# New tables of steps for a group's slots and for the prologue's sums, another order at the beginning, and the last low part of h ahead of the first output tile

## The chip, the cores and the metric

The kernel runs on one core of one Trainium2 chip. The metric is the device time of one execution in microseconds (us). Five engines work side by side, each through its own queue of instructions in program order: TensorE (PE, matmuls), VectorE (DVE), ScalarE (ACT), GpSimd (POOL) and SyncE (SP, which here issues every DMA). An instruction that waits holds up all that stands behind it on its engine.

## The reference

```python
xn = layernorm(x)                                  # x: 2048 x 576
q, k, v = split(xn @ wqkv)                         # 32 heads of 18
scores = q @ k.T * 18 ** -0.5                      # a key counts if 0 <= i - j < 256
s = (softmax(scores) @ v) @ wo
h = (xn @ w_gate) * (xn @ w_up)                    # 4608 columns
g = silu(h @ w_down)
out = x + s * g
```

All of it is float32.

## The kernel before

Each float32 operand is split into a high and a low float16 part, and each product is made of three passes (high x high, high x low, low x high). In the code `hi` writes a high part (ACT) and `lo` a low part (DVE). The parts are scaled by powers of two that come from the largest values.

**The prologue** (about 0 to 178 us). Sixteen tiles of 128 rows of x are normalised: `stats` (DVE), `root` (ACT), `newton` (DVE), then `norm2` (two ACT steps, then two POOL steps in `parts`), then `turn`, a transposing DMA into XT. Tile 0 goes another way: PE transposes it, ACT copies it (`turned`), POOL makes its low part (`turned_low`). `v_pass(t, i0, i1)` makes passes i0 to i1 of the fourteen that give v for tile t, and `v_out` reads them out. The weights of v lie in `rv` (raw) and `wv` (high parts 0 to 4, low parts 5 to 9). The weights of q and k arrive in `rqk` in five blocks. Their largest value `am_qk` is spread over the partitions through PE (`spread_pe`, `spread_pe2`), and `qk_scale` and `qk_split` make the parts that the tiles of q and k (`qk_tile`, L387) need. All this is done for rows 0 to 1023 and then for 1024 to 2047.

**The main part** (about 178 to 1511 us). It has 18 groups of four slots. A group holds 256 of the 4608 columns; a slot works on 512 rows. In a slot, PE makes seven sums of products (q = 0 to 6, L1159, a fast scheme in which sums and differences of blocks of the weights, `tw`, and of x, `sx`, save an eighth of the matmuls), 92 matmuls in 16 places. `h_hi` and `h_lo` split h, the product of both branches, into `hh`. `down` 0 to 4 (L1023) multiplies the h of the slot before by w_down. A step of attention runs in every slot from slot 1 to slot 64, some of it in the slots after: `score` (DVE), `shifted` and `probs` (ACT), `turn_probs` (the low part of the probabilities, then one transposing DMA to `pt`), `weigh` (PE, L940), `finish` (DVE), `finish2` (POOL), `store_o`. `turn_probs(i)` comes in two halves, j = 0 and 1, and the DMA goes out with the second. For the first 16 steps the window has fewer keys.

In each group the weights of the next one are made ready: `ffn_raw` (loads), `ffn_amax` (ACT), the scales, `up_hi`/`up_lo`, `dn_hi`/`dn_lo`/`dn_low`, `wd_sum`/`wd_hi`/`wd_lo`, and `t_sum` (POOL), `t_hi` (ACT), `t_lo` (DVE), which make `tw`.

**What sets the order.** The schedule is written by hand. `at(slot, place, f, ...)` puts a step on a list, and `at_place` issues the steps of a place in the order of their entry, with `score_pairs` and `down` first. In every slot, `seven_place` issues the matmuls of the place before that. The table `AT` gives the places, counted from the first slot of a group (or from the step's own slot) in units of a sixteenth of a slot; a number above 15 lies in a later slot. Negative numbers, relative to slot 0, lie in the prologue's second half.

`AT["p"]` has, for each slot of a group and each of eight quarters of a step, the places of `score`, `shifted`, `probs`, `turn_probs` and `weigh`. `AT["en"]` says for each slot which of ten steps run on DVE (1) rather than POOL (0): the two products of `seven_mult`, then the eight `turn_probs`. `AT["eng"][4]` says where `dn_low` runs, ACT (1) or POOL (0). `AT["on"]` says the same (DVE or POOL) for the steps of `sx`, `AT["sx"]` their places; `t0`, `u0`, `wd0` and `g0` are the places for group 0, made in the prologue.

In the last slot the second part of h is special:

```python
at(sl, (17, 18)[ft] if last else AT["h"][sl % NCH][1][ft], h_lo, sl, ft)
...
at(NSLOT, 1, o_out, 0)
```

so the last two `h_lo` are at places 1 and 2 after the last slot. `o_out(t)` makes output tile t: a silu on ACT (L1250), 28 matmuls (L1262), two DVE steps that read them (L1264), an addition and a store.

Of the kernel before, what the change touches and what calls it, by code (L numbers as in the profile page):

```python
# [13 lines left out]
OP = mybir.AluOpType  # L14
# [6 lines left out]
def kernel(  # L21
# [23 lines left out]
    scale = DH ** -0.5  # L45
# [143 lines left out]
    def hi(w, rv, s):  # L189
        nc.scalar.activation(w, rv, AF.Copy, scale=s)  # L190
# [92 lines left out]
    def turn(t):  # L283
        nc.sync.dma_start(XT[:, :, t * 128:(t + 1) * 128], XN.pop(t), transpose=True)
# [464 lines left out]
    for k in range(3, 5):  # L749
        raw_wide(rqk, wqkv, 0, 2 * D, k)  # L750
# [18 lines left out]
    turned_low(0, nc.gpsimd)  # L769
# [513 lines left out]
    at(NSLOT, 1, o_out, 0)  # L1283
# [41 lines left out]
```

## Time and profile before

| | us |
|---|---|
| runs of the kernel, median (lowest to highest of 3) | 1578.68 (1578.66 to 1579.19) |
| the profiled execution, its own time | 1580.56 |
| its span, first to last instruction | 1578.8 |
| PE busy | 1556.4 (99%) |
| DVE busy | 1268.3 (80%) |
| ACT busy | 1069.4 (68%) |
| POOL busy | 847.7 (54%) |

The granted clock of TensorE was 0.999 over the span. The profile gives one execution. A row of a timeline holds the start, the time taken, the engine, the source line, the operation, out<-in, shapes and count. In brackets follows the idle time of the engine just before it and what ended that. A busy PE is not PE at its peak, since matmuls are pipelined and each record covers the pipeline too. In the chain of work a row holds start, time and what it was. PE reads no waits of its own from a table: only where its row has a bracket did it stand still.

### The profile page before, as it was taken

To read this page: it belongs to the slowest core of one execution; us is meant where nothing else is said; L and a number is where in the kernel's file an instruction comes from. 1 tells how busy PE (TensorE), PEld (TensorE's weight loads), DVE (VectorE), ACT (ScalarE), POOL (GpSimd) and SP (SyncE) were. 2 spreads that over 40 slices of the span, in tenths; PEclk is the share of its full clock that TensorE was granted. 3 is DMA by queue.
4 is the path that set the end of the run, shared out by engine and by line. 5 is a ranking of instruction groups with operands and counts; after the bars stand their busy time and mean duration, and the time that the engine had idled before them with its cause. 6 is when DMAs were issued, how large, how long until landed. Compare 5 with 4: busy or idle time off the path is not lost.

```text
span 1578.8 us, 40055 instructions
## 1 busy us (share of the span) xinstructions
PE 1556.4 (99%) x15498; PEld 1106.7 (70%) x15498; DVE 1268.3 (80%) x2752; ACT 1069.4 (68%) x1853; POOL 847.7 (54%) x1064
## 2 busy tenths in 40 slices
PE   8999999999999999999999999999999999999999
PEld 5465577777777776777777777777777777777767
DVE  7537688888888988898889888888888888877654
ACT  6435478777777877777778787878777777752230
POOL 4126355657464757575766666566757575732000
PEclk9999999999999999999999999999999999999999
DMA  9583436565557687777777676767686868651238
GB/s 233 190 246 129 166 73 138 96 129 107 122 106 143 122 146 137 130 143 135 145 122 152 121 155 119 154 121 149 118 158 123 155 120 149 122 98 38 63 82 220
DMA packets 566575, 212.14 MB, mean 134 GB/s; under 512 B 504560, under 2 KB 544624, under 8 KB 566384
## 3 DMA queue, kind: packets, MB, share of 16 engines
q1 hardware_dynamic: 566384, 209.58, 64.2%
q8 instruction: 121, 1.98, 0.6%
q14 instruction: 70, 0.57, 0.1%
HBM read 76.63 MB, written 29.00 MB: 67 GB/s over the span
## 4 chain that ended last, share of the span: by engine, by line
PE 83%; DVE 6%; POOL 4%; DMA 3%; ACT 2%; issue 2%; SPq 1%; DVEq 0%; POOLq 0%; ACTq 0%
PE up L1159 40%; PE dn L1023 21%; PE s L387 4%; PE pv L940 3%; PE up L1112 3%; PE s L896 2%; PE s L1023 2%; PE s L1262 2%; DMA pt<-pp 2%; PE up L1262 2%; PE up L387 1%; POOL pp L928 1%; DVE hh L1007 1%; POOL tf L507 1%; PE s L338 1%
## 5 line engine op out<-in xcount | busy, mean ns | idle before, releaser
L1023 PE MATMUL dn<-dnw,hh 128*128 128x512 f16 (+1 forms) x3168 | 444.7, 286 | 1.2
L1159 PEld LDWEIGHTS <-tw 128*128 128x128 f16 x3456 | 320.2, 98 | 62.1 <-DVE tw L193 5.1
L1023 PEld LDWEIGHTS <-hh 128*128 128x128 f16 x3456 | 222.2, 98 | 170.8 <-issue 19.2
L1159 PEld LDWEIGHTS <-upw 128*128 128x128 f16 x3024 | 283.8, 98 | 64.5 <-issue 22.2
L1129 DVE SCALAR_TENSOR_TENSOR gt<-up,gt 128x512 f32<-128x512 f32 x360 | 247.7, 688 | 62.4 <-PE up L1112 40.3
L1030 DVE SCALAR_TENSOR_TENSOR acc<-dn,sc,acc 128x512 f32<-128x512 f32 x310 | 215.3, 694 | 99.2 <-PE dn L1023 99.0
L1159 PE MATMUL up<-XT,upw 128*128 128x256 f16 x2160 | 276.6, 273 | 0.0
L915 ACT ACTIVATE mx<-mx,sig 128x2 f32<-128x2 f32 x256 | 98.1, 383 | 217.5 <-DVE mx L907 217.5
L1159 PE MATMUL up<-XT,tw 128*128 128x256 f16 x1728 | 236.0, 273 | 2.5 <-DVE gt L1129 2.5
L1159 PE MATMUL up<-sx,tw 128*128 128x256 f16 x1728 | 225.0, 273 | 2.4 <-DVE tw L193 2.4
L1134 POOL TENSOR_TENSOR ht<-gt 128x512 f32<-128x512 f32 x72 | 92.0, 1278 | 94.7 <-DVE gt L1129 93.9
L940 PEld LDWEIGHTS <-pt 128*128 128x128 f16 x2880 | 109.5, 96 | 41.1 <-DMA pt<-pp 6.3
L940 PE MATMUL pv<-vt,pt 128*128 128x37 f16 x2880 | 112.9, 179 | 4.5 <-DMA pt<-pp 4.5
L1159 PE MATMUL up<-sx,upw 128*128 128x256 f16 x864 | 112.7, 273 | 0.0
L1125 ACT ACTIVATE gt<-up 128x512 f32<-128x512 f32 x144 | 83.7, 581 | 30.9 <-PE up L1159 17.3
L1001 ACT ACTIVATE hh<-ht 128x512 f16<-128x512 f32 x72 | 45.2, 627 | 67.4 <-POOL ht L1134 67.4
L507 POOL TENSOR_TENSOR tf<-raw 128x256 f32<-128x256 f32 x102 | 83.0, 814 | 0.1
L507 POOL TENSOR_TENSOR tf<-raw,tf 128x256 f32<-128x256 f32 x68 | 62.0, 913 | 21.8 <-DVE tw L193 21.8
L193 DVE SCALAR_TENSOR_TENSOR upw<-raw,sc,upw 128x640 f16<-128x640 f32 x72 | 71.9, 1001 | 0.0
L315 ACT ACTIVATE upw<-raw 128x1280 bf16<-128x1280 f32 (+1 forms) x51 | 62.5, 1225 | 3.8 <-DMA raw<-in_B_w_up_dram 3.7
L193 DVE SCALAR_TENSOR_TENSOR tw<-tf,sc,tw 128x512 f16<-128x512 f32 x68 | 49.5, 749 | 14.5 <-ACT tw L190 13.7
L896 PE MATMUL s<-ks,qs 54*128 54x384 f16 (+2 forms) x512 | 60.2, 312 | 0.0
(1353 smaller groups left out, 2918.3 us busy)
## 6 DMA issues: line engine op xcount, KB each, us to landing
raw<-in_B_w_down_dram SPq DMA_DIRECT2D x36, 288.0 KB
qk_d<-qp SPq DMA_DIRECT2D x18, 512.0 KB
raw<-in_B_w_gate_dram SPq DMA_DIRECT2D x36, 256.0 KB
raw<-in_B_w_up_dram SPq DMA_DIRECT2D x36, 256.0 KB
ks<-qk_d SPq DMA_DIRECT2D x96, 81.0 KB
qs<-qk_d SPq DMA_DIRECT2D x128, 54.0 KB
vt<-v_d SPq DMA_DIRECT2D x48, 111.0 KB
qk_d<-qp SPq DMA_DIRECT2D x20, 256.0 KB
```

What stands on the lines that cost most here:

```text
L193: nc.vector.scalar_tensor_tensor(w, rv, s, h, op0=OP.mult, op1=OP.subtract)
L387: nc.tensor.matmul(ps, a, b, start=i == 0 and not opened, stop=i == 12 and opened)
L507: nc.gpsimd.tensor_tensor(t[:, to], x0, x1, op=OP.subtract)
L896: nc.tensor.matmul(ps[:, :hi_ - lo_], QS[s][r, i * 128:(i + 1) * 128], KS[s][r, lo_:hi_], start=True, stop=True)
L915: nc.scalar.activation(mx[:, 1], mx[:, 0], AF.Identity, bias=sig[:, 2:3], scale=sig[:, 1:2])
L940: nc.tensor.matmul(PVB[s][:, j, i, :VW], pt[:, nb * j + n + n // nb * nb], VT[s][:, lo_ + n % nb, j * VW:(j + 1) * VW], start=n == 0, stop ...
L1023: nc.tensor.matmul(to, a, b, start=q == 0, stop=q == len(l) - 1)
L1030: nc.vector.scalar_tensor_tensor(d, src, SC[g][:, 9:10], d, op0=OP.mult, op1=OP.add)
L1125: nc.scalar.activation(seven_new(sl, name), CH[q], AF.Copy, scale=H_SC)
L1129: nc.vector.scalar_tensor_tensor(seven_new(sl, name), CH[q], H_SC, x, op0=OP.mult, op1=OP.add)
L1134: eng.tensor_tensor(HT[sl, f], u[:, 0], u[:, 1], op=OP.mult)
L1159: nc.tensor.matmul(CH[q][:, o], a, b, start=CH["first"], stop=last and q not in (1, 2, 5), skip_group_check=q in ON)
```

## The change

Nearly all entries of `AT` are changed. Those that the steps below speak of, old above new (for `p`, the places of `turn_probs` and `weigh` are the last two of five; only rows of slot 0 and 1 of a group are shown):

```diff
-           "dn": ((41, 45), (51, 52), (52, 48)),
+           "dn": ((37, 45), (51, 54), (52, 48)),
-           "down": ((6, 9, 12, 15, 20), (6, 8, 11, 14, 16), (6, 8, 11, 14, 16), (6, 9, 12, 15, 19)),
+           "down": ((6, 9, 12, 15, 21), (6, 8, 11, 14, 16), (6, 8, 11, 14, 16), (6, 9, 12, 15, 18)),
-           "en": ((0, 1, 0, 0, 0, 0, 1, 0, 0, 0), (0, 1, 0, 0, 0, 0, 1, 0, 0, 0),
-                  (0, 1, 0, 0, 0, 0, 1, 0, 0, 0), (0, 1, 0, 0, 0, 0, 1, 0, 0, 0)),
+           "en": ((0, 1, 0, 0, 0, 0, 0, 1, 0, 0), (0, 1, 0, 0, 0, 0, 1, 1, 0, 0),
+                  (0, 1, 0, 0, 0, 0, 1, 1, 0, 0), (0, 1, 0, 0, 0, 0, 1, 1, 0, 0)),
-           "end": ((30, 32, 35), (28, 32, 33), (28, 32, 33), (28, 32, 33)),
+           "end": ((29, 31, 32), (30, 33, 35), (28, 32, 35), (28, 30, 33)),
-           "eng": (1, 1, 0, 1, 1, 0, 1, 0, 0, 0, 0, 0, 0, 1),
+           "eng": (1, 1, 1, 1, 0, 0, 0, 0, 1, 0, 1, 0, 1, 1),
-           "h": (((15, 17), (18, 21)), ((15, 17), (19, 21)), ((15, 17), (21, 21)), ((15, 17), (19, 21))),
+           "h": (((15, 17), (18, 19)), ((15, 19), (19, 21)), ((15, 17), (20, 21)), ((15, 17), (21, 21))),
-           "p": (((6, 7, 8, 11, 22), (6, 7, 8, 12, 22), (7, 8, 12, 13, 22), (7, 8, 12, 13, 23),
-                  (13, 14, 15, 18, 24), (13, 14, 15, 19, 24), (13, 15, 20, 21, 30), (15, 17, 20, 21, 30)),
-                 ((6, 7, 8, 11, 22), (6, 7, 8, 12, 22), (7, 8, 12, 13, 22), (7, 8, 12, 13, 23),
-                  (13, 14, 15, 18, 24), (13, 14, 15, 19, 24), (13, 15, 20, 21, 28), (15, 17, 20, 21, 28)),
+           "p": (((6, 7, 8, 13, 20), (6, 7, 9, 13, 21), (7, 8, 12, 13, 21), (7, 8, 12, 13, 22),
+                  (13, 14, 15, 18, 25), (13, 14, 15, 19, 25), (13, 15, 20, 21, 29), (15, 17, 20, 21, 29)),
+                 ((6, 7, 8, 11, 22), (6, 7, 8, 12, 22), (7, 8, 10, 13, 24), (7, 8, 10, 13, 25),
+                  (13, 14, 15, 18, 26), (13, 14, 15, 19, 26), (13, 15, 20, 21, 30), (15, 17, 20, 21, 30)),
...
-           "raw": (8, 9, 12, 16, -6, 0),
+           "raw": (7, 9, 16, 17, -5, -1),
-           "sum": ((30, 36, 50, 59, 64), (41, 53, 56, 61, 62)),
+           "sum": ((32, 39, 46, 59, 67), (43, 53, 56, 61, 62)),
-           "t_hi": ((57, 57), (67, 69)),
+           "t_hi": ((57, 57), (70, 70)),
-           "u0": ((-9, -8, -7, -7), (-7, -7, -7, -4)),
+           "u0": ((-9, -8, -7, -7), (-7, -7, -7, -1)),
-           "up_lo": (41, 40, 65, 62),
+           "up_lo": (41, 40, 64, 62),
-           "wd": ((55, 56), (65, 69), (70, 74)),
+           "wd": ((55, 56), (65, 71), (69, 74)),
```

`amax`, `g0`, `load`, `scale`, `sx`, `on`, `t0`, `up_hi` and `wd0` change too, most by one or two places, with a few steps of `sx` on the other of their two engines. The beginning:

```diff
     for k in range(2, 5):
         hi(wv[:, k], rv[:, k], ps_v[:, 2:3])
+    nc.gpsimd.tensor_scalar(rv[:, 0], rv[:, 0], ps_v[:, 2:3], None, op0=OP.mult)
+    nc.gpsimd.tensor_tensor(wv[:, 5], rv[:, 0], wv[:, 0], op=OP.subtract)
     newton(2, 1, 1)
     norm2(3)
     turn(3)
+    stats(4)
+    stats(5)
+    root(4, 2)
     for k in range(1, 3):
         raw_wide(rqk, wqkv, 0, 2 * D, k)
...
-    turned(0, x32[:, 0:4], x32[:, 4])
...
-    stats(4)
-    lo(wv[:, 5], rv[:, 0], ps_v[:, 2:3], wv[:, 0])
-    stats(5)
-    root(4, 2)
+    newton(4, 2)
     lo(wv[:, 6], rv[:, 1], ps_v[:, 2:3], wv[:, 1])
-    newton(4, 2)
     for t in range(4, 6):
         norm2(t)
         turn(t)
-    for k in range(3, 5):
-        raw_wide(rqk, wqkv, 0, 2 * D, k)
...
     stats(6)
+    root(6, 1)
+    newton(6, 1)
+    norm2(6)
+    turn(6)
+    for k in range(3, 5):
+        raw_wide(rqk, wqkv, 0, 2 * D, k)
     v_out(0)
     stats(7)
-    root(6, 2)
+    root(6, 1, 1)
     v_pass(3, 0, 14)
-    newton(6, 2)
-    norm2(6)
-    turn(6)
-    amax(am_qk[:, 0:1], rqk[:, 0])
     v_out(1)
+    newton(6, 1, 1)
     norm2(7)
     turn(7)
+    amax(am_qk[:, 0:1], rqk[:, 0])
+    turned(0, x32[:, 0:4], x32[:, 4])
     turned_low(0, nc.gpsimd)
```

The largest value of q's and k's weights is now spread during `v_pass(7)` (after passes 2 and 5) instead of during `v_pass(6)` (after passes 9 and 12). And at the end:

```diff
-    at(NSLOT, 1, o_out, 0)
+    at(NSLOT, 2, o_out, 0)
```

With that, `o_out(0)` comes after both `h_lo` and after `down` 4 of the slot before the last.

More of the change, by code (lines that the diff above doesn't have):

```diff
@@ L66 @@
     LEAST, MOST = 2.0 ** -60, 2.0 ** 60
-    AT = {"amax": (19, 20, 6),
-           "dn": ((41, 45), (51, 52), (52, 48)),
-           "down": ((6, 9, 12, 15, 20), (6, 8, 11, 14, 16), (6, 8, 11, 14, 16), (6, 9, 12, 15, 19)),
-           "en": ((0, 1, 0, 0, 0, 0, 1, 0, 0, 0), (0, 1, 0, 0, 0, 0, 1, 0, 0, 0),
-                  (0, 1, 0, 0, 0, 0, 1, 0, 0, 0), (0, 1, 0, 0, 0, 0, 1, 0, 0, 0)),
-           "end": ((30, 32, 35), (28, 32, 33), (28, 32, 33), (28, 32, 33)),
-           "eng": (1, 1, 0, 1, 1, 0, 1, 0, 0, 0, 0, 0, 0, 1),
-           "g0": (-22, -19, -22, -21, -9, -16, -14, -11, -11),
-           "h": (((15, 17), (18, 21)), ((15, 17), (19, 21)), ((15, 17), (21, 21)), ((15, 17), (19, 21))),
-           "load": (8, 3, 15),
-           "mult": {1: 6, 4: 18, 5: 1, 6: 0},
[12 rows of a table removed]
-           "pairs": (6, 13),
-           "raw": (8, 9, 12, 16, -6, 0),
-           "scale": (26, 28, 35, 51),
-           "sum": ((30, 36, 50, 59, 64), (41, 53, 56, 61, 62)),
[5 rows of a table removed]
-           "t_hi": ((57, 57), (67, 69)),
-           "t_lo": ((57, 58), (70, 71)),
-           "u0": ((-9, -8, -7, -7), (-7, -7, -7, -4)),
-           "up_hi": (36, 36, 60, 61),
-           "up_lo": (41, 40, 65, 62),
-           "wd": ((55, 56), (65, 69), (70, 74)),
-           "wd0": ((-4, 3), (-1, 4), (-1, 7))}
@@ new lines @@
+    AT = {"amax": (18, 20, 6),
+           "dn": ((37, 45), (51, 54), (52, 48)),
[4 more added lines that the diff above has]
+           "eng": (1, 1, 1, 1, 0, 0, 0, 0, 1, 0, 1, 0, 1, 1),
+           "g0": (-22, -22, -20, -23, -10, -15, -14, -11, -11),
+           "h": (((15, 17), (18, 19)), ((15, 19), (19, 21)), ((15, 17), (20, 21)), ((15, 17), (21, 21))),
+           "load": (7, 3, 14),
+           "mult": {1: 6, 4: 20, 5: 1, 6: 0},
[12 rows of a table added]
+           "pairs": (6, 13),
+           "raw": (7, 9, 16, 17, -5, -1),
+           "scale": (25, 28, 35, 50),
+           "sum": ((32, 39, 46, 59, 67), (43, 53, 56, 61, 62)),
[5 rows of a table added]
+           "t_hi": ((57, 57), (70, 70)),
+           "t_lo": ((57, 58), (70, 71)),
+           "u0": ((-9, -8, -7, -7), (-7, -7, -7, -1)),
+           "up_hi": (37, 37, 61, 61),
+           "up_lo": (41, 40, 64, 62),
+           "wd": ((55, 56), (65, 71), (69, 74)),
+           "wd0": ((-4, 0), (-1, 6), (-1, 7))}
@@ L779 @@
         if t % 8 > 3 or t >= 8:
-            v_pass(t, 0, 9)
-            if t == 6:
+            v_pass(t, 0, 2)
+            if t == 7:
                 spread_pe(am_qk[:, 5:6], 1, "s", 4)
-            v_pass(t, 9, 12)
-            if t == 6:
+            v_pass(t, 2, 5)
+            if t == 7:
                 tp = spread_pe2(1, "s", 4)
-            v_pass(t, 12, 14)
-            if t == 6:
                 qk_scale(tp)
+            v_pass(t, 5, 14)
             if t == 6:
```

26 rows, old and new, of the table AT are left out of this document.

## The prediction

> **What bounds the kernel now.** I read the page first, then who makes PE wait, then the chain of work, then the timelines of single engines at each place where PE waits.
>
> ```profile
> span 1578.8 us, 40055 instructions
> PE 1556.4 (99%) x15498; PEld 1106.7 (70%) x15498; DVE 1268.3 (80%) x2752; ACT 1069.4 (68%) x1853; POOL 847.7 (54%) x1064
> ```
>
> PE runs one fixed stream of matmuls, and the change leaves their number alone. So the change can only move the time through the gaps in that stream. Who made PE wait (total us, times, longest):
>
> ```profile
> PE pv L940 <- DMA pt<-pp: 4.5, 5, 1.1
> PE up L1159 <- DVE gt L1129: 2.5, 2, 2.1
> PE up L1159 <- DVE tw L193: 2.4, 8, 0.4
> PE s L1023 <- DVE hh L1007: 1.5, 2, 1.3
> ```
>
> These idle times are lower bounds. A matmul's record covers its pipeline, so the loss in cadence is some 0.15 us more for each wait. The waits fall in four places: the beginning (its rows follow), one wait of 2.1 us in the first slot, the first of the four slots of a group (tw, pt, and a little hh), and the last slot (the 1.3 of hh). In the chain of work the same 36 matmuls of slot 2 recur:
>
> ```profile
> 1034.48 3.93 PE up L1159 x36
> 1110.06 3.93 PE up L1159 x36
> 45.61 11.22 PE s L387 x52
> 33.03 4.98 DMA XT<-xh
> ```
>
> A group takes 1110.06 - 1034.48 = 75.58 us. One 512-column matmul takes 11.22/52 = 0.216 us. "Same" below means within 0.2% (3.2 us), about what a measurement of this kernel tells from no change.
>
> **The beginning.** PE, DVE, SP and POOL between 18 and 40 us:
>
> ```profile
> 23.82 0.41 PE L338 MATMUL up<-wv,XT 128*128 128x288 f16 x2 [1.34 <-DVE wv L193]
> 29.68 3.60 PE L338 MATMUL s<-wv,XT 128*128 128x288 f16 x28 [0.56 <-DVE sm L262]
> 38.06 2.38 PE L338 MATMUL s<-wv,XT 128*128 128x288 f16 x18 [1.35 <-DMA XT<-xh]
> 22.96 1.54 DVE L193 SCALAR_TENSOR_TENSOR wv<-rv,ps_v,wv 128x576 f16<-128x576 f32 x2
> 26.22 2.87 SPq L284 DMA_TRANSPOSE XT<-xh  x2
> 29.14 0.58 SPq L197 DMA_DIRECT2D rqk<-in_A_wqkv_dram  x1
> 21.16 1.27 POOL L735 TENSOR_TENSOR wv<-rv,wv 128x576 f16<-128x576 f32 x1
> 39.09 0.15 DVE L804 TENSOR_REDUCE am_qk<-am_qk 128x1 f32<-128x5 f32 x1
> ```
>
> Three waits can go: 1.34 + 0.56 + 1.35 = 3.25 us idle, some 3.7 in cadence.
>
> First, PE waits at 23.82 for the low parts of `wv` that start at 22.96. The change takes `lo(wv[:, 5])` (half of that row's two: 0.77 us) off DVE's queue ahead of them, and the rest of that queue (statistics 4 and 5, `newton(4,2)`, the low part of `wv[:, 6]`) is only put in another order. They should come 0.8 to 1.3 us earlier, the upper end if the rows beside POOL's 1.27 are not stretched as now.
>
> POOL gets two operations for it. One like the row of L735 is 1.27 us; the scaling before it is bounded by the same row and by twice that. They fit between POOL's work on tiles 2 and 3 and cost nothing there. Without that cover tile 3 would be late by 1.3 us.
>
> Second, ACT drops the three copies of `turned(0)` from the stretch ahead of tiles 4 and 5, and their statistics are taken sooner. Their normalisation, and the transposes of 26.22, move forward by about 2 us, which ends the wait of 29.68 (an XT tile, I read it, though the view names DVE).
>
> Third, `turn(6)` is now issued ahead of the loads of `rqk` 3 and 4 (29.14 on) instead of behind them. In the chain it is the 4.98 us transfer that PE meets at 38.06, and it should now land before it is wanted.
>
> What is late next: tile 7. Its `norm2` stands behind `v_out(1)` and its transpose behind the two moved loads. I expect it to land near 38.5 to 39.5, against about 38 when PE could want it (tile 6 starts at 38.06 and takes 3.6, less the 3.7 won), so PE waits about 1 us there. Then `am_qk`: before, it was ready at 39.2. With `rqk` 3 and 4 loaded later and `turned(0)` now on ACT ahead of its squares, I expect 39.5 to 40. The change moves its consumer to tile 7, so nine passes of matmuls still cover it.
>
> Sum: 3.7 less about 1.5 = **-2.2 us**, so L387 starts near 43.4 instead of 45.61. Bounds: -4 (no new wait) to +1 (`am_qk` 3 us late). The first slot's wait stays as it is:
>
> ```profile
> 186.03 2.59 PE L1159 MATMUL up<-XT,tw 128*128 128x256 f16 x12 [2.11 <-DVE gt L1129]
> ```
>
> DVE's queue ahead of that read (`dn_lo`, three steps of `sx` for c = 2, one split) keeps its order in the new tables: 0. The step of c = 3 that leaves DVE for POOL, and `up_lo` 3 that comes in at place -1, both lie before an idle stretch of DVE.
>
> **Slot 0 of a group.** Twelve groups lose time here (eight tw waits and four of the five pt waits). One of them:
>
> ```profile
> 998.54 0.48 DVE L1030 SCALAR_TENSOR_TENSOR acc<-dn,sc,acc 128x256 f32<-128x256 f32 x1 [0.27 <-PE dn L1023]
> 998.94 1.12 DVE L928 TENSOR_TENSOR pp<-sm__16025,pp 128x384 f16<-128x384 f32 x1
> 999.99 1.40 DVE L1007 SCALAR_TENSOR_TENSOR hh<-hh,ht 128x512 f16<-128x512 f16 x1
> 1001.31 0.68 DVE L1007 SCALAR_TENSOR_TENSOR hh<-hh,gt 128x512 f16<-128x512 f16 x1
> 999.61 1.23 POOL L928 TENSOR_TENSOR pp<-sm__16025,pp 128x384 f16<-128x384 f32 x1
> 1000.73 1.75 PE L1023 MATMUL dn<-dnw,hh 128*128 128x512 f16 x6
> 1038.99 1.47 PE L1023 MATMUL dn<-dnw,hh 128*128 128x512 f16 x6
> 1004.42 0.35 DVE L193 SCALAR_TENSOR_TENSOR wd<-raw,sc,wd 64x128 f16<-64x128 f32 x1
> 1006.55 0.38 PE L1159 MATMUL up<-sx,tw 128*128 128x256 f16 x2
> 1007.23 0.61 PE L1159 MATMUL up<-sx,tw 128*128 128x256 f16 x4 [0.30 <-DVE tw L193]
> ```
>
> The six matmuls take 1.75 against 1.47 in slot 2: 0.28 lost to `h_lo`. The two at 1006.55 end their issue 2 x 0.11 (3.93/36) later, so the next should start at 1006.77, not 1007.23: 0.46 lost to `t_lo`. With a small follower that is some 0.85 us a group.
>
> The new table puts the second half of `turn_probs(2)` on DVE (now POOL, 1.23 us). It also puts `wd_lo` 0 (0.35) ahead of `h_lo`, and brings `down` 4 one place earlier, which takes DVE's 0.27 of waiting away. Ahead of `h_lo` DVE gains one 128x384 subtraction and 0.35. Beside POOL that subtraction took 1.12, and `h_lo` took 1.40 instead of 0.68.
>
> With POOL's piece gone from that moment, 0.72 comes back on `h_lo` and about 0.4 on the subtraction beside it. So +0.7 (estimate: 1.12 less the 0.4) + 0.35 - 0.27 - 0.72 - 0.4 = about -0.3: `h_lo` no later, slightly earlier. The Trainium skill, "SBUF — State Buffer", section "Who interferes with whom", says that a VectorE instruction with two SBUF inputs and a GpSimd instruction that reads SBUF exclude each other for the whole of whichever began first. The two rows agree (DVE's 1.40 covers the rest of POOL's 1.23 and then its own 0.68), and by the rule moving the piece off POOL is worth slightly more than I take.
>
> Behind `h_lo`, `t_lo` loses the 0.35 of `wd_lo` that stood before it. `t_hi` of both kinds, now at place 6 after ACT's copy, still ends about 1003.2, before DVE wants it. So `t_lo` comes 0.38 earlier or more.
>
> I take **-0.55 us a group, 12 groups: -6.6**; bounds -0.9 and, if DVE is late, +1.0 each. The groups with a pt wait show this:
>
> ```profile
> 627.00 0.47 PE L940 MATMUL pv<-vt,pt 128*128 128x37 f16 x12 [1.04 <-DMA pt<-pp]
> 620.62 2.22 SPq L931 DMA_TRANSPOSE pt<-pp  x1
> ```
>
> The transpose goes out when POOL's piece has ended. On DVE that end is about 0.6 earlier, the same gain. The fifth pt wait is in slot 1, where `weigh(2)` moves one place later: **-0.5**.
>
> **Slots 1 to 3.** These now have slack and lose some. `turn_probs` on DVE rises by one in slots 2 and 3.
>
> ```profile
> 1038.37 0.69 DVE L1007 SCALAR_TENSOR_TENSOR hh<-hh,gt 128x512 f16<-128x512 f16 x1
> 1056.97 0.68 DVE L1007 SCALAR_TENSOR_TENSOR hh<-hh,gt 128x512 f16<-128x512 f16 x1
> 1057.64 1.47 PE L1023 MATMUL dn<-dnw,hh 128*128 128x512 f16 x6
> 1054.91 1.53 DVE L193 SCALAR_TENSOR_TENSOR dnw<-raw,sc,dnw 128x576 f16<-128x576 f32 x2
> L1134 POOL TENSOR_TENSOR ht<-gt 128x512 f32<-128x512 f32 x44 | 55.9, 1271 | 4.1 <-DVE gt L1129 3.3 <-DMA raw<-in_B_w_gate_dram 0.8
> ```
>
> The second `h_lo` ends at 1039.06 in slot 2, and its first matmul (the sixth) is due at 1038.99 + 5 x 0.216 = 1040.07: slack 1.0. In slot 3 it is 1058.72 - 1057.65 = 1.07. The added subtraction is 0.5 to 1.1. In slot 3 one of the two `dn_lo` (1.53/2 = 0.77) moves behind `h_lo` and pays for it.
>
> `dn_low` (two a group) moves from ACT to POOL. Nothing of before shows it there; by size the row of L1134 gives 1.27 x 576/512 = 1.43, and a smaller tile gives less. Its cover is POOL's idle time, and its danger is that DVE waits beside it. In slot 1 `weigh(1)` comes a place earlier, closer to its transpose. I allow **+1.5 us** over all groups; bounds 0 (the slack holds) to +15 (the first rival below has the mechanism: some 1.2 us in each of 12 groups).
>
> **The end.**
>
> ```profile
> 1516.70 0.52 DVE L1264 SCALAR_TENSOR_TENSOR acc<-dn,sig,acc 128x288 f32<-128x288 f32 x1 [2.09 <-ACT acc L1250]
> 1518.35 0.69 DVE L1007 SCALAR_TENSOR_TENSOR hh<-hh,gt 128x512 f16<-128x512 f16 x1
> 1519.09 4.97 PE L1023 MATMUL s<-dnw,hh 128*128 128x512 f16 x43 [1.27 <-DVE hh L1007]
> ```
>
> The last `h_lo` starts at 1518.35 because it is queued on DVE behind `o_out(0)`, whose first step waited 2.09 us for ACT. With `o_out(0)` at place 2, `h_lo` 1 comes first, ends near 1515.4, and `o_out(0)`'s matmuls and `down` 4 cover it. The whole of PE's wait (1.3 us idle, 1.4 in cadence) goes, and all behind it is PE: **-1.4**, within 0.3.
>
> **Sum.** -2.2 + 0 - 6.6 - 0.5 + 1.5 - 1.4 = -9.2 us. The profiled execution took 1580.56 (span 1578.8), so it would be 1571.4. The median of the runs is 1578.68, 1.9 lower, so I forecast 1569.5.
>
> **Rivals.**
>
> *DVE becomes the bound (slower).* The subtraction costs its 1.12, `dn_low` on POOL blocks DVE in slot 3 for up to 2 x 1.43, and `h_lo` comes later than the slack. It decides where the second `h_lo` ends more than 1.07 us later in slot 3, or 1.0 in slot 2. For: DVE has no idle time there now. Against: POOL gives up a piece of 1.23 in each of those slots. At a net loss of 1.0 (1.43 less the 0.4 of a shorter subtraction, roughly) in 12 groups: +12 - 2.2 - 1.4 = +8.4, about 1587.
>
> *The beginning is bound by its transfers, and slot 0 gives half.* The same bytes must land before L387. Then 0 at the beginning, -3.3, -0.5, -1.4: -5.2, 1573.5.
>
> *The tables only move the waits.* Slots 1 to 3 lose what slot 0 gains, and the beginning nothing: -1.4 alone, 1577.3.
>
> *All waits go.* 12 x 0.95 (0.85, and more where pt is waited for), 1.1 in slot 1, 4 at the beginning and 1.4 at the end: -17.9, 1560.8.
>
> **Chances.** My forecast 0.62, all waits go 0.07, half 0.10, moved waits 0.08, DVE bound 0.13. The first three are faster by over 0.2%: 0.79. Moved waits: 0.08 same. DVE bound: 0.13 slower. Range 1561 to 1578: it leaves out the slower rival and little of the rest.
>
> **What would show it.** Right: L387 starts at 43 to 44; the group period falls from 75.58 to about 75.0; no tw wait among PE's; the waits for pt shrink; no hh wait of 1.3 at the end. Wrong: waits of L1023 for hh in slots 2 or 3, or new waits for pt in slot 1, or L387 at 45 or later. A DVE `turn_probs` of 1.2 us and more beside POOL would point to the slower rival.

## Result and profile after

| | before | changed |
|---|---|---|
| median (lowest to highest), 14 runs each, same chip | 1579.05 (1578.12 to 1579.99) | 1580.53 (1579.22 to 1581.81) |
| profiled execution, own time / span | 1580.56 / 1578.8 | 1579.22 / 1577.2 |
| DVE / POOL / ACT busy | 1268.3 / 847.7 / 1069.4 | 1293.7 / 871.9 / 1051.6 |

The ratio is 1.0008, 95% interval 1.0001 to 1.0016: no change by the bound of 0.2%, and if anything 1.5 us slower. Forecast were 1569.5 us and a range of 1561 to 1578: the prediction was wrong. The two profiled executions stand the other way round (1.3 us in favour of the changed kernel). That of before is 1.5 us above its median and holds five waits for `pt`; that of the changed kernel is the fastest of its runs. So stages are compared below, not spans. From line 804 on the changed kernel's line numbers are one higher (L1023 is L1024, L1159 is L1160).

DVE's share of the chain of work rose from 6% to 12%. Who made PE wait (total us, times, longest):

```profile
PE dn L1024 <- DVE hh L1008: 7.9, 24, 0.5
PE up L1160 <- DVE gt L1130: 4.0, 3, 2.9
```

The waits for tw and for `pt` are gone, and so is the last one for hh. In their place stand 24 waits for hh in the first slot of a group, two in each of twelve groups: the two `h_lo`. The chain of work gives the group period and the start of L387:

```profile
45.32 11.22 PE s L387 x52
1033.39 3.93 PE up L1160 x36
1109.23 3.93 PE up L1160 x36
```

A group takes 75.84 us, against 75.58 before (seven of the last twelve groups before were as free of other waits as that one; the five others took 75.70 to 76.91). Forecast was 75.0. This is slot 0 of that group in the changed kernel, in four engines' timelines:

```profile
997.16 1.80 DVE L929 TENSOR_TENSOR pp<-sm__16030,pp 128x384 f16<-128x384 f32 x2
998.99 0.35 DVE L193 SCALAR_TENSOR_TENSOR wd<-raw,sc,wd 64x128 f16<-64x128 f32 x1
999.38 0.69 DVE L1008 SCALAR_TENSOR_TENSOR hh<-hh,ht 128x512 f16<-128x512 f16 x1
999.98 1.40 DVE L1008 SCALAR_TENSOR_TENSOR hh<-hh,gt 128x512 f16<-128x512 f16 x1
1001.49 0.69 DVE L1130 SCALAR_TENSOR_TENSOR gt<-up,gt 128x512 f32<-128x512 f32 x1
997.50 1.05 POOL L507 TENSOR_TENSOR tf<-raw 128x256 f32<-128x256 f32 x1
999.71 2.46 POOL L929 TENSOR_TENSOR pp<-sm__16034,pp 128x384 f16<-128x384 f32 x2 [1.16 <-ACT pp L923]
998.80 0.83 ACT L923 CAST pp<-sm__16034 128x768 f16<-128x768 f32 x1
999.37 0.60 PE L1024 MATMUL dn<-dnw,hh 128*128 128x512 f16 x2
1000.12 0.82 PE L1024 MATMUL dn<-dnw,hh 128*128 128x512 f16 x3 [0.15 <-DVE hh L1008]
1001.45 0.39 PE L1024 MATMUL dn<-dnw,hh 128*128 128x512 f16 x1 [0.50 <-DVE hh L1008]
```

Read it from PE upwards. The sixth matmul of `down` 0 was due at 999.37 + 5 x 0.216 = 1000.45 and started at 1001.45. It waits for the second `h_lo`, which took 1.40 us instead of 0.69. That step stood on DVE while POOL did the next piece, `turn_probs(3,0)`, from 999.71. Before, POOL began that piece 1.5 us later, counted from the start of `down` 0 (999.37 here), since ACT's `probs(3)` stood behind a `t_hi` that waited 0.70 for POOL's `t_sum`; now its cast ends at 998.80 + 0.83 = 999.63. The two rows of before, where `down` 0 began at 1000.73:

```profile
999.68 0.72 ACT L190 ACTIVATE tw<-tf,sc 128x512 f16<-128x512 f32 x1 [0.70 <-POOL tf L507]
1002.54 1.79 POOL L928 TENSOR_TENSOR pp<-sm__16029,pp 128x384 f16<-128x384 f32 x2 [1.71 <-ACT pp L922]
```

So the piece that left POOL (`turn_probs(2,1)`) was followed by another one, which has come forward.

### The profile page after: what moved, and what is told of

Its sections match the earlier page's. It is cut to its first block, busy times and chain, and to the rows that moved or that the text cites. A ratio compares the mean times of both kernels' runs of the same rounds, so it can differ in the third digit from the quotient of the medians.

```text
span 1577.2 us, 39934 instructions
## 1 busy us (share of the span) xinstructions
PE 1555.0 (99%) x15498; PEld 1105.4 (70%) x15498; DVE 1293.7 (82%) x2805; ACT 1051.6 (67%) x1818; POOL 871.9 (55%) x1053
## 4 chain that ended last, share of the span: by engine, by line
PE 81%; DVE 12%; ACT 3%; issue 2%; DVEq 0%
PE up L1160 38%; PE dn L1024 21%; PE pv L941 4%; PE s L387 4%; PE up L1113 2%; PE s L1024 2%; PE s L897 2%; PE s L1263 2%; DVE hh L1008 2%; PE up L1263 2%; PE up L387 1%; DVE acc L1031 1%; DVE pp L929 1%; DVE upw L193 1%; DVE gt L1130 1%
## 5 line engine op out<-in xcount | busy, mean ns | idle before, releaser
L1024 PE MATMUL dn<-dnw,hh 128*128 128x512 f16 (+1 forms) x3168 | 446.9, 287 | 7.9 <-DVE hh L1008 7.9
L1160 PEld LDWEIGHTS <-tw 128*128 128x128 f16 x3456 | 319.3, 97 | 59.7 <-issue 4.8
L1024 PEld LDWEIGHTS <-hh 128*128 128x128 f16 x3456 | 222.3, 98 | 178.8 <-DVE hh L1008 20.3
L1160 PEld LDWEIGHTS <-upw 128*128 128x128 f16 x3024 | 283.5, 98 | 59.9 <-issue 17.3
L1130 DVE SCALAR_TENSOR_TENSOR gt<-up,gt 128x512 f32<-128x512 f32 x360 | 247.6, 688 | 66.2 <-PE up L1113 48.1
L1160 PE MATMUL up<-XT,upw 128*128 128x256 f16 x2160 | 275.8, 273 | 0.0
L1160 PE MATMUL up<-XT,tw 128*128 128x256 f16 x1728 | 227.9, 272 | 4.0 <-DVE gt L1130 4.0
L1160 PE MATMUL up<-sx,tw 128*128 128x256 f16 x1728 | 230.6, 272 | 0.0
L941 PE MATMUL pv<-vt,pt 128*128 128x37 f16 x2880 | 118.2, 180 | 0.0
L1160 PE MATMUL up<-sx,upw 128*128 128x256 f16 x864 | 112.5, 273 | 0.0
L507 POOL TENSOR_TENSOR tf<-raw 128x256 f32<-128x256 f32 x102 | 94.7, 929 | 0.5 <-DVE sc L447 0.5
L607 POOL TENSOR_SCALAR dnw<-dnw 128x576 f16<-128x576 f16 x36 | 61.4, 1705 | 13.4 <-ACT dnw L190 13.4
L507 POOL TENSOR_TENSOR tf<-raw,tf 128x256 f32<-128x256 f32 x68 | 57.1, 840 | 18.8 <-DVE tw L193 18.7
L1008 DVE SCALAR_TENSOR_TENSOR hh<-hh,ht 128x512 f16<-128x512 f16 x72 | 60.8, 845 | 0.6
```

The source lines that it names most:

```text
L507: nc.gpsimd.tensor_tensor(t[:, to], x0, x1, op=OP.subtract)
L941: nc.tensor.matmul(PVB[s][:, j, i, :VW], pt[:, nb * j + n + n // nb * nb], VT[s][:, lo_ + n % nb, j * VW:(j + 1) * VW], start=n == 0, stop ...
L1008: nc.vector.scalar_tensor_tensor(b, a, -LO, h, op0=OP.mult, op1=OP.add)
L1024: nc.tensor.matmul(to, a, b, start=q == 0, stop=q == len(l) - 1)
L1130: nc.vector.scalar_tensor_tensor(seven_new(sl, name), CH[q], H_SC, x, op0=OP.mult, op1=OP.add)
L1160: nc.tensor.matmul(CH[q][:, o], a, b, start=CH["first"], stop=last and q not in (1, 2, 5), skip_group_check=q in ON)
```

## Experiments

Each run's difference is its median less that of the kernel before, run beside it on the same chip. The period is the difference of two x36 rows of the chain, one group apart, as above; for the kernels with the old tables, where single groups differ, it is the mean of ten groups (before: (1337.24 - 578.46)/10 = 75.88).

| run | us to before | ratio, 95% interval | group period |
|---|---|---|---|
| changed kernel | +1.5 | 1.0008 (1.0001 to 1.0016) | 75.84 |
| only the tables | +1.5 | 1.0013 (1.0004 to 1.0022) | 1109.92 - 1034.07 = 75.85 |
| only the beginning | +1.1 | 1.0007 (0.9999 to 1.0016) | (1335.70 - 578.40)/10 = 75.73 |
| only the end | -1.4 | 0.9993 (0.9984 to 1.0002) | (1336.69 - 579.24)/10 = 75.75 |
| `turn_probs(2,1)` back on POOL | +3.6 | 1.0022 (1.0013 to 1.0032) | 1112.75 - 1036.97 = 75.78 |
| `probs(3)` later | +4.4 | 1.0028 (1.0018 to 1.0038) | 1112.95 - 1037.35 = 75.60 |
| `h_lo` earlier | -1.9 | 0.9991 (0.9982 to 0.9999) | 1109.01 - 1033.55 = 75.46 |
| `wd_lo` 0 behind `h_lo` | -6.4 | 0.9960 (0.9946 to 0.9974) | 1105.03 - 1029.91 = 75.12 |
| `wd_lo` 0 behind `t_lo` too | -7.4 | 0.9952 (0.9938 to 0.9965) | 1106.46 - 1031.34 = 75.12 |
| the same, `weigh(2)` and `dn_lo` of the first group later | -1.1 | 0.9992 (0.9983 to 1.0001) | 1111.87 - 1036.75 = 75.12 |
| `wd_lo` 0 behind `t_lo`, `weigh(2)` and scores of slot 0 later | -12.3 | 0.9921 (0.9909 to 0.9934) | 1100.76 - 1026.15 = 74.61 |
| the same and POOL's `wv` 9 later | -12.1 | 0.9925 (0.9912 to 0.9939) | 1099.76 - 1025.15 = 74.61 |
| the same and `wv` 9 on DVE | -13.8 | 0.9911 (0.9897 to 0.9924) | 1100.37 - 1025.76 = 74.61 |

### Which part is it

Tables alone (all of `AT`, nothing else):

> The kernel before with only the new tables (beginning and end in the old order). Theory A (the whole loss is in slot 0 of the groups; the wait for hh grows by 0.7, the tw wait of 0.46 goes): group period 75.84 in all twelve groups, and the median 2 to 4 us above before. Prediction's term: -5.6 (slot 0, slot 1 and the allowance). Rival C (the tables gain and the beginning loses): 3 us or more below before.

Measured +1.5, period 75.85, and the same 24 waits for hh of 7.9 us. So the tables alone are as much slower as the whole change. Theory A holds in the trace (75.84 or 75.85 in each of the twelve groups); the time is a little under its 2 to 4.

The beginning alone (the program order shown in the change, old tables, old end):

> The kernel before with only the new program order of the beginning (all tables and the end as before). Theory A (the waits at the beginning are exchanged for others of the same length: the wait for the first low parts of wv stays, tile 4's transpose comes late because parts(4) on POOL starts late): within 1 us of before. My prediction's term: -2.2 us. Rival C (the beginning costs time and hides a gain of the tables): +3 us or more.

Measured +1.1, with no change just inside the interval. The -2.2 is not there.

The end alone:

```diff
-    at(NSLOT, 1, o_out, 0)
+    at(NSLOT, 2, o_out, 0)
```

> The kernel before with only o_out(0) at place 2 after the last slot instead of place 1. Both theories: -1.4 us, PE's last wait for hh of 1.3 us gone and nothing in its place. If the wait only moves into the output tiles (DVE's first step waits for ACT's silu in any case): 0.

Measured -1.4, as forecast; its interval just reaches no change, but the trace of the changed kernel shows it too:

```profile
1514.70 0.68 DVE L1008 SCALAR_TENSOR_TENSOR hh<-hh,gt 128x512 f16<-128x512 f16 x1
1516.37 6.04 PE L1024 MATMUL s<-dnw,hh 128*128 128x512 f16 x48
```

The last `h_lo` ends at 1515.38, a microsecond before its matmuls, and no bracket follows them. The three parts sum to 1.5 + 1.1 - 1.4 = +1.2; the whole measured +1.5.

### Why h_lo is late

Order on DVE:

```diff
-           "wd": ((55, 56), (65, 71), (69, 74)),
+           "wd": ((55, 56), (65, 71), (70, 74)),
```

> The changed kernel with wd_lo 0 at place 6 of slot 0 instead of place 5, so that it stands behind the two h_lo on DVE instead of ahead of them. Theory A (the second h_lo is late because 0.35 us of wd_lo stand ahead of it and POOL's turn_probs(3,0) then begins before it): the second h_lo starts 0.05 us ahead of POOL's piece or so, takes 0.7 instead of 1.41 and PE's wait for hh of 0.98 a group falls to 0.3 or less: 12 x 0.7 = 8 us less than the changed kernel, 6.5 less than before. If POOL still wins the race, only 0 to 2 us less. Rival B (DVE has too much work in slot 0, whatever its order: what h_lo gains, the read behind it or t_lo loses): within 1.5 us of the changed kernel.

Measured -6.4 to before, 8 below the changed kernel: theory A to the figure. Its timelines of DVE, POOL and PE:

```profile
1071.84 0.68 DVE L1008 SCALAR_TENSOR_TENSOR hh<-hh,gt 128x512 f16<-128x512 f16 x1
1072.06 2.12 POOL L929 TENSOR_TENSOR pp<-sm__17364,pp 128x384 f16<-128x384 f32 x2 [1.16 <-ACT pp L923]
1071.73 1.47 PE L1024 MATMUL dn<-dnw,hh 128*128 128x512 f16 x6
1077.78 0.61 PE L1160 MATMUL up<-sx,tw 128*128 128x256 f16 x4 [0.20 <-DVE tw L193]
```

A step of 0.35 us is worth 0.72 a group, since with it gone the second `h_lo` begins 0.2 us ahead of POOL's piece instead of 0.27 behind. The six matmuls take the undisturbed 1.47. A wait for tw of 0.20 has come back.

POOL's piece held back, DVE's queue as in the changed kernel:

```diff
-                  ..., (13, 15, 21, 22, 28), (15, 17, 21, 22, 28))),
+                  ..., (13, 15, 22, 23, 28), (15, 17, 22, 23, 28))),
```

> The changed kernel with probs(3,0) and (3,1) of the last slot's step one place later (place 6 of slot 0, behind ACT's copy) and the turn_probs after them, so that POOL begins its subtraction about 2.5 us later, after h_lo. Nothing on DVE's queue is changed. Theory A (POOL's subtraction holds the second h_lo up for 0.72 us): h_lo takes 0.69 us twice, PE's wait for hh falls from 0.98 to 0.2 or 0.3 a group; POOL's pieces then stand beside t_lo and may give back 0.1 to 0.4 there: 3 to 8 us less than the changed kernel. Rival B (DVE's amount of work): within 1.5 us of the changed kernel, the second h_lo as late as before.

Two rows of slot 0 in a late group and two in an early one:

```profile
1004.21 0.68 DVE L1008 SCALAR_TENSOR_TENSOR hh<-hh,gt 128x512 f16<-128x512 f16 x1
1007.21 1.22 DVE L193 SCALAR_TENSOR_TENSOR tw<-tf,sc,tw 128x512 f16<-128x512 f32 x1
257.77 0.42 DVE L908 CUSTOM_DVE_ANT_0 sm__3100<-s,bias 128x256 f32<-128x256 f32 x1 [0.81 <-POOL pp L929]
259.26 0.61 PE L1160 MATMUL up<-sx,tw 128*128 128x256 f16 x4 [0.52 <-DVE tw L193]
```

The cause is shown: with POOL idle beside it, the second `h_lo` takes 0.68. But the time is a miss: POOL's pieces now stand beside `t_lo` (1.22 instead of 0.74), so a late group gains only 0.24. In the first four groups, where nothing was waited for, a score now waits for its buffer until POOL is done; such a group went from 72.74 to 73.94. Hence +4.4, not the gain that theory A gave.

The subtraction put back on POOL:

```diff
-                  ..., (0, 1, 0, 0, 0, 0, 1, 1, 0, 0)),
+                  ..., (0, 1, 0, 0, 0, 0, 1, 0, 0, 0)),
```

> The changed kernel with turn_probs(2,1) of the last slot's step back on POOL, as before; all else as changed. It tests whether moving that subtraction to DVE paid. Theory A (POOL's pieces and DVE's two-input steps take turns, so that DVE gains the 1.08 us of the subtraction and then loses it waiting for POOL's (2,1) and (3,0)): h_lo ends no earlier, PE's hh wait stays at 0.6 to 1.2 us, within 4 us of the changed kernel on either side, and pt waits come back. My prediction's step (POOL's piece out of the way is worth 0.72 + 0.4 against 0.7): 3 to 6 us slower than the changed kernel. Rival B (the amount of work on DVE is all): 12 x 0.9 = 10 us less than the changed kernel.

```profile
1002.37 1.29 DVE L1008 SCALAR_TENSOR_TENSOR hh<-hh,ht 128x512 f16<-128x512 f16 x1
1003.58 1.40 DVE L1008 SCALAR_TENSOR_TENSOR hh<-hh,gt 128x512 f16<-128x512 f16 x1
1005.03 0.39 PE L1024 MATMUL dn<-dnw,hh 128*128 128x512 f16 x1 [0.50 <-DVE hh L1008]
```

DVE has a subtraction less (1.08 beside POOL) and both `h_lo` are stretched instead, by 0.6 and 0.7. The same wait of 0.50 results, and the same period: moving this subtraction to DVE, the heart of the forecast for slot 0, was worth nothing (75.84 against 75.78). So the amount of work on DVE alone does not explain it, and neither does POOL's piece alone. The rows fit that the two engines' steps take turns, and that their sum ahead of `h_lo` counts. (Against the changed kernel it is 2.1 us slower, since the first four groups lose 0.8 each.)

`h_lo` ahead of the second subtraction:

```diff
-                  ..., ((15, 17), (21, 21))),
+                  ..., ((15, 17), (19, 19))),
```

> The changed kernel with both h_lo of the last slot of a group at place 3 of slot 0 instead of place 5: on DVE they come behind turn_probs(2,0) and ahead of turn_probs(2,1) and wd_lo 0. Theory A (order on DVE and POOL's subtraction make h_lo late): h_lo end near 999.5 instead of 1001.4 (in the clock of the changed kernel's profile), no wait for hh in slot 0; turn_probs(2,1) ends about 1 us later and its pt is still in time, the read of sum 2 waits as before (0.1): 12 x 0.8 to 1.0 = 9 to 12 us less than the changed kernel, 8 to 10 less than before. Rival B (DVE's amount of work): the wait comes back at the read of sum 2 (up <- gt) or at pt, gain under 2 us.

```profile
1000.74 0.89 DVE L193 SCALAR_TENSOR_TENSOR wd<-raw,sc,wd 64x128 f16<-64x128 f32 x1
1000.24 2.17 POOL L929 TENSOR_TENSOR pp<-sm__16034,pp 128x384 f16<-128x384 f32 x2 [1.15 <-ACT pp L923]
1002.40 0.60 PE L1160 MATMUL up<-XT,tw 128*128 128x256 f16 x4 [0.59 <-DVE gt L1130]
```

The hh waits are gone, but POOL now stretches `wd_lo`, the read of sum 2 (L1130) comes late behind it, and PE waits 0.59 there. The gain of 3.4 to the changed kernel lies between theory A (9 to 12) and rival B (under 2), and the wait came back where rival B had put it: another order inside a full stretch moves the wait.

### What is left in slot 0

`wd_lo` 0 further back, at place 8:

```diff
-           "wd": ((55, 56), (65, 71), (69, 74)),
+           "wd": ((55, 56), (65, 71), (72, 74)),
```

> The changed kernel with wd_lo 0 at place 8 of slot 0: behind h_lo and behind both t_lo as well (place 6, the experiment before, put it behind h_lo but ahead of the two t_lo, where PE then waited 0.2 us for tw in nine groups). Theory A (what stands ahead of the step that PE waits for next is what counts): the hh wait stays gone, the tw wait goes too, a group takes 74.6 instead of 75.13, so 12 x 0.4 to 0.5 = 5 to 6 us less than with place 6, about 1567, 12 less than before; waits for pt may keep 1 to 3 of it. Rival B (DVE's amount of work is the bound of slot 0): the 0.35 comes back as a longer wait at the read of sum 3 (up <- gt), 1572 as with place 6.

```profile
1003.93 0.69 DVE L1130 SCALAR_TENSOR_TENSOR gt<-up,gt 128x512 f32<-128x512 f32 x1
1004.68 0.92 PE L1160 MATMUL up<-XT,tw 128*128 128x256 f16 x7 [0.37 <-DVE gt L1130]
```

Here theory A fell: the tw wait went, but the read of sum 3 (L1130) now stands behind the 0.35, PE waits 0.37 for it, and the period stayed at 75.12. Between `h_lo` and that read DVE had no room. So the next run (with `weigh(2)` of the last slot's step at place 11 instead of 10 as well) took work out of the stretch:

```diff
-                  ..., (7, 8, 12, 13, 21), (7, 8, 12, 13, 22),
+                  ..., (9, 10, 12, 13, 21), (9, 10, 12, 13, 22),
```

> The changed kernel with wd_lo 0 at place 8, weigh(2) of the last slot's step at place 11, and the two scores of the second pair in slot 0 (1.1 us on DVE) at place 9, behind the read of sum 3, instead of place 7. It asks what the 0.5 us is that a group still loses with wd_lo out of the way (period 75.13). Theory D (between h_lo and the read of sum 3 DVE has more work than the time there: only taking work out of that stretch helps, not another order inside it): the wait of 0.36 us for gt goes, a group takes 74.6, 12 x 0.5 and about 1 us of pt waits less than with place 8 alone, about 1565 to 1566, 13 below before. Rival E (the read is late for POOL's subtractions or for PE's own sum, not for DVE's work): 1572 as before. If the scores that come later hold up the probabilities, new waits for pt in slot 1 would take some of it back.

```profile
996.49 1.41 DVE L193 SCALAR_TENSOR_TENSOR tw<-tf,sc,tw 128x512 f16<-128x512 f32 x2
998.32 0.69 DVE L1130 SCALAR_TENSOR_TENSOR gt<-up,gt 128x512 f32<-128x512 f32 x1
```

1566.51 us, 12.3 below before. No wait is left in slot 0, and a group takes 74.61. The next run, which has `weigh(2)` later as well but not the scores, keeps 75.12, so the 0.51 is the scores'. Theory D is shown.

An attempt at the first slot's wait, two `dn_lo` of the first group eight places later, beside place 8 for `wd_lo` and place 11 for `weigh(2)`:

```diff
-            at(b, AT["dn"][1][k] if g else 65 + k, dn_lo, g, k)
+            at(b, AT["dn"][1][k] if g else 73 + k, dn_lo, g, k)
```

> An attempt at a version better than both. The changed kernel with wd_lo 0 at place 8 of slot 0, weigh(2) of the last slot's step one place later (place 11), and the two dn_lo of the first group, which stand ahead of the read of sum 2 in the first slot, eight places later. Theory A: as the run with place 8 alone, less 1.5 us for waits on pt and less 1.5 in the first slot, whose wait of 2.85 us for gt should fall to about 1.4 (ACT's copy, which the read needs too, ends 1.5 us before the read started): about 1564. Rival: the first slot's wait is bound by something else and stays (1566).

```profile
PE up L1160 <- DVE gt L1130: 8.8, 15, 4.2
```

A miss. The wait for sum 2 fell only from 2.85 to 1.9, and the moved steps held up the sums of x behind them: a new wait of 4.2 us early in the second slot.

### The beginning

In the kernel before, PE's first matmul with `wv`:

```profile
16.26 2.37 PE L338 MATMUL up<-wv,XT 128*128 128x288 f16 x18 [0.41 <-DVE wv L723]
```

The changed kernel, PE, DVE, POOL and SP:

```profile
15.71 2.37 PE L338 MATMUL up<-wv,XT 128*128 128x288 f16 x18 [0.42 <-DVE wv L723]
22.75 0.40 PE L338 MATMUL up<-wv,XT 128*128 128x288 f16 x2 [1.32 <-DVE wv L193]
30.21 3.77 PE L338 MATMUL s<-wv,XT 128*128 128x288 f16 x28 [1.43 <-DMA XT<-xh]
20.58 1.20 DVE L262 SCALAR_TENSOR_TENSOR sm<-sm 128x2 f32<-128x2 f32 x1
29.51 0.94 DVE L348 SCALAR_TENSOR_TENSOR vo<-s,ps_v,vo 128x288 f16<-128x288 f32 x2 [2.10 <-ACT vo L347]
20.48 1.28 POOL L738 TENSOR_TENSOR wv<-rv,wv 128x576 f16<-128x576 f32 x1
25.46 6.42 SPq L284 DMA_TRANSPOSE XT<-xh  x3
```

From that matmul to L387 it was 45.61 - 16.26 = 29.35 us and is 45.32 - 15.71 = 29.61. One wait went (1.35 at 38.06), one kept its length (1.32), one grew (0.56 to 1.43). (The 6.42 of the SP row runs to the end of tile 6's transpose, which went out only at 30.59; the first two took 1.69 and 1.89.) A step of `newton(4,2)` on two numbers per partition takes 1.20 us beside POOL's subtraction, and the low parts of `wv` and tile 4's whole chain stand behind it.

The wait that grew has a second cause. The matmuls at 30.21 write the buffers `s` that `v_out(0)` reads (L348), and the new order issues `v_out(0)` behind tile 6's normalisation: the read began at 26.61 before and begins at 29.51 now. In this profile the row names the transpose, but in eight of the ten other runs with the new beginning it names that read. In the run of the beginning alone the weight load that needs XT started at 29.96 and the matmul at 30.21, 0.57 after the read began.

The step beside POOL was tried on the kernel with the later scores: POOL's subtraction was moved behind tiles 4 and 5:

```diff
-    nc.gpsimd.tensor_tensor(wv[:, 9], rv[:, 4], wv[:, 4], op=OP.subtract)
...
     for t in range(4, 6):
         norm2(t)
         turn(t)
+    nc.gpsimd.tensor_tensor(wv[:, 9], rv[:, 4], wv[:, 4], op=OP.subtract)
```

> The kernel of the run beside it (second pair of scores at place 9) and, at the beginning, POOL's subtraction for wv 9 moved behind its work on tiles 4 and 5. In the changed kernel it took POOL 20.48 to 21.76, and DVE's step of newton(4,2) that started at 20.58, 0.17 us elsewhere, ended at 21.77. Theory A (a POOL step that reads SBUF holds a DVE step with two SBUF inputs up for its whole length): newton(4,2) ends 1.0 us earlier, the low parts of wv and tile 4's transpose with it, PE's wait of 1.32 us for wv falls to 0.3 and the wait for XT behind it stays, so -1.0 us against the run beside it. Rival F (DVE's steps there are slow for another cause, or the transposes bound the beginning whatever DVE does): the step stays at 1.2 us, or it falls and the XT wait grows by as much; 0.

```profile
20.62 0.16 DVE L262 SCALAR_TENSOR_TENSOR sm<-sm 128x2 f32<-128x2 f32 x1
21.76 0.41 PE L338 MATMUL up<-wv,XT 128*128 128x288 f16 x2 [0.33 <-DVE wv L193]
27.10 0.41 PE L338 MATMUL up<-wv,XT 128*128 128x288 f16 x2 [3.23 <-POOL wv L747]
```

The step fell to 0.16 and the first wait to 0.33, so the cause of that wait is shown; but the part moved was itself wanted at 23.9, a new wait of 3.23, and nothing was won. Last, the same low part as a fourth DVE step of the kind that stands there anyway:

```diff
-    nc.scalar.activation(rv[:, 4], rv[:, 4], AF.Copy, scale=ps_v[:, 2:3])
-    nc.gpsimd.tensor_tensor(wv[:, 9], rv[:, 4], wv[:, 4], op=OP.subtract)
...
-    for k in range(2, 4):
+    for k in range(2, 5):
         lo(wv[:, 5 + k], rv[:, k], ps_v[:, 2:3], wv[:, k])
```

> The kernel with the second pair of scores at place 9, and at the beginning the low part of wv's last block made by DVE in one step behind the three it makes anyway, in place of ACT's scaling and POOL's subtraction (which, moved behind tiles 4 and 5, had become a wait of 3.23 us itself). Theory A (POOL's subtraction stretches newton(4,2) by 1.0 us; with it gone, and the last low part in time, everything behind it comes 1.0 us earlier): DVE's step of L262 at 0.17 us, PE's first wait for wv 0.3 instead of 1.30, the wait for XT behind it 1.3 as before, 1.0 us less than with the scores alone, about 1565.5. Rival F (the three transposes, which take 6.4 us together, bound that place): the first wait falls by 1.0 and the XT wait grows by as much, 1566.5.

```profile
16.08 2.37 PE L338 MATMUL up<-wv,XT 128*128 128x288 f16 x18 [0.48 <-DVE wv L723]
22.09 0.41 PE L338 MATMUL up<-wv,XT 128*128 128x288 f16 x2 [0.30 <-DVE wv L193]
29.94 3.89 PE L338 MATMUL s<-wv,XT 128*128 128x288 f16 x28 [1.36 <-DVE vo L348]
45.16 11.22 PE s L387 x52
```

45.16 - 16.08 = 29.08, half a microsecond better than 29.61, where theory A gave 1.0. The first wait is at its 0.30, but the other 0.5 is lost behind `v_out(0)`, which the row of 29.94 names: the weight load with XT started at 29.44, the matmul at 29.94. From the start of that read to L387 it is 15.8 us in the changed kernel, in the run of the beginning alone, with the later scores and here. No run moved `v_out(0)` by itself, so that it sets the beginning is read from the traces and not shown by an experiment. The median, 1565.35, is 1.2 below that of the later scores alone (on another chip, and their ranges overlap), but 13.8 below before: the fastest version here.

## Why the prediction was wrong

**The step that failed** is in slot 0: "With POOL's piece gone from that moment, 0.72 comes back on `h_lo`". The mechanism was the right one and was applied to one piece only. POOL's next piece, `turn_probs(3,0)`, had been held back by ACT's `t_hi`; the prediction noted that `t_hi` is now at place 6, and did not ask what ACT and POOL do earlier for that. The second `h_lo` lost its 0.71 to the new neighbour, just what the first one won. The two subtractions ahead took 1.80 (POOL's `t_sum` beside them) against the one of 1.12, so the second cost 0.68 where 0.7 - 0.4 = 0.3 was forecast, and `wd_lo` cost its 0.35. With the 0.27 of waiting gone, as forecast, that is 0.68 + 0.35 - 0.27 = +0.76 instead of -0.3; the second `h_lo` ends 2.01 behind the start of `down` 0 now, and ended 1.26 behind it before. The loss to hh, in cadence (from start to start of the matmuls), was 0.28 before and is (1000.12 - 999.37 - 2 x 0.216) + (1001.45 - 1000.12 - 3 x 0.216) = 0.32 + 0.68 = 1.00 now. With the tw wait of 0.46 gone, as forecast, that is 1.00 - 0.28 - 0.46 = +0.26 a group, as 75.84 against 75.58 has it. Forecast was -0.55, so such a group is 0.8 off.

In the profile of before, the five groups of 75.70 to 76.91 had other waits, and those went too. So over the twelve groups (502.51 to 1411.93, against 502.88 to 1412.16, both starts of the 36 matmuls of slot 2) the changed kernel is only 0.1 us slower in these two profiles. The two runs with the old tables and a new beginning or end took 907.9 and 908.1 there, 1.3 to 1.5 less than its 909.4. Forecast for these groups was -6.6 - 0.5 + 1.5 = -5.6, so they hold some 6 to 7 of the error of 11.0, and the beginning 2.5.

The page of the Trainium skill, "SBUF — State Buffer", section "Who interferes with whom", was applied rightly as far as it went, and it agrees with the runs wherever POOL subtracts: a DVE step with two SBUF inputs waits out POOL's step (0.69 to 1.40, 0.16 to 1.20), whereas the reads of L1130, which have one input in PSUM, took 0.69 beside the same POOL piece. (Beside `dn_low`, which does not subtract, a DVE step with two SBUF inputs was held up for part of POOL's step only; see the first slot.) The error was to price the piece that leaves and not the one that takes its place.

**Beginning, -2.2:** the low parts were to come 0.8 to 1.3 earlier. They did not, since the same stretch (1.20 on a step of `newton(4,2)`) is on the new queue too, and that queue now has `newton(4,2)` ahead of `wv[:, 6]`, for which PE now waits. The second wait was to vanish; tile 4's transposes went out at 25.46 against 26.22, only 0.2 earlier once the start (0.55) is taken off, and `v_out(0)`, for whose later place the prediction put nothing, would have held PE until about then too. The third went, and tile 7 and `am_qk` cost next to nothing. Sum +0.26 by the trace. The rival "bound by its transfers" had the right figure for another reason.

**First slot, 0:** the queue kept its order but not its lengths. The first DVE step of `dn_lo` before, then the same step, POOL's two `dn_low` and PE's wait in the changed kernel:

```profile
180.99 0.81 DVE L193 SCALAR_TENSOR_TENSOR dnw<-raw,sc,dnw 128x576 f16<-128x576 f32 x1
```

```profile
180.69 1.27 DVE L193 SCALAR_TENSOR_TENSOR dnw<-raw,sc,dnw 128x576 f16<-128x576 f32 x1
180.69 3.41 POOL L607 TENSOR_SCALAR dnw<-dnw 128x576 f16<-128x576 f16 x2 [13.45 <-ACT dnw L190]
186.47 1.47 PE L1160 MATMUL up<-XT,tw 128*128 128x256 f16 x12 [2.85 <-DVE gt L1130]
```

The wait grew from 2.11 to 2.85; what this cost is in the last section. `dn_low` on POOL takes 3.41/2 = 1.7 us here, not the 1.43 estimated; it stretched DVE's two steps by 0.46 and 0.39 (1.21 against 0.82), less than its own length.

**Slots 1 to 3, +1.5:** nothing was lost; the 24 hh waits are all in slot 0. The lower bound was right. **pt and the end:** as forecast (no pt wait in the profile, -1.4).

Of the rivals, "the tables only move the waits" came nearest in time (1577.3), with the place wrong: slot 0 lost what slot 0 gained.

**Open:** the medians of the tables alone (+1.5) and of the beginning alone (+1.1) each have an interval of 0.2%, and single executions of the old tables differ by some 1.5 us over ten groups (758.78 and 757.30 in two profiles), whose groups meet different waits for pt and tw. The first slot adds nothing or up to 0.8 from one execution to the next (last section). So how the last microsecond divides between them isn't settled.

## What to carry to other kernels

When a step is moved off an engine to clear the way for another, look for what that engine does next and what had held it back: the change may call it forward into the same gap. Where two engines take turns, fill the stretch ahead of each wait by the sum of both, and take out of it what nobody waits for yet; 0.35 us of such work was worth 8 us, and two scores put behind a read another 5 or 6. And shift work only past the reader that needs it: two of the misses here were steps put off a little too far.

## What the runs showed of the hardware

After PE's wait of 2.1 to 2.9 us in the first slot the granted clock sometimes halves for some microseconds. Before, and the changed kernel, 186 to 190 us (the last three columns are granted clock, DMA share and GB/s):

```profile
186.00:190.00 4.00, 3.97 (x22) 2.93 (x22) 3.55 (x7) 2.26 (x4) 1.25 (x1) 0.57 0.28 84
```

```profile
186.00:190.00 4.00, 2.82 (x25) 2.38 (x25) 3.78 (x7) 2.47 (x5) 1.46 (x2) 1.00 0.34 118
```

Twelve matmuls took 2.59 us before (as quoted in the prediction) and 1.47 in the changed kernel, so in this execution its longer wait cost nothing. In the run with `wd_lo` behind `h_lo` a wait of 2.86 was followed by 0.62 in the same stretch. Of all profiles, the three with the wait of 2.11 show a clock of 0.57 to 0.60 there and the one with 1.91 shows 0.62; of the ten with 2.85 or 2.86, four show 0.62 to 0.78 and six 1.00. From the last 52 matmuls of L387 (149.37 in the changed kernel) to the 36 of slot 2 in the first group (211.39) it is 62.0 us in the three with 2.11 and in the six with the long wait and the full clock, and 62.5 to 62.8 in the four others: there the longer wait costs 0.5 to 0.8. The Trainium skill, "TensorE: Matmul & The Clock Gate", section "Part 1: The HAM clock gate (the "warmup" mystery)", has the clock halved after an idle window of some 3.4 us that runs free of the program. A free-running window would fit that the same wait is followed now by the one clock and now by the other; but here 2.11 us of waiting were enough, less than its window. No run here varied the wait alone, so what decides it stays open.
